# Attention and a tanh-shrink layer on one core: the projection by seven half-size products from tile 6 on, and 25 other constants of a hand-planned schedule

## The chip, the cores and the metric

The kernel runs on one core of a Trainium2 chip. A core has TensorE (PE in the profile; PEld is its weight load, which overlaps the products), VectorE (DVE), ScalarE (ACT), GpSimd (POOL) and SyncE (SP), which run at the same time and wait for each other by semaphores. SP, ACT and POOL also issue DMA transfers, each over a ring (queue) of its own. The metric is the device time of one execution in microseconds; the time of a kernel is the median of its runs.

## What is computed

Four batches of eight heads, 768 tokens, 64 numbers a head. Half of the heads (the retrieval heads; which ones is an input) attend causally to all earlier tokens, the others to the first 4 tokens and a window of 64. The result is a matrix x of 3072 tokens by 512, which passes through a layer of width 2048:

```
scores = scale * np.matmul(q, k.transpose(0, 1, 3, 2))
...
a = np.exp(scores)
a = a / (np.sum(a, axis=-1, keepdims=True) + 1e-09)
return np.matmul(a, v).astype(np.float32)
...
h = x @ w_in
g = h - np.tanh(h)
return (g @ w_out).astype(np.float32)
```

Everything comes in and goes out in 32-bit floats; the kernel computes its products in 16-bit floats with 32-bit sums.

## The kernel before, in words

**Tiles.** The 3072 tokens are 12 tiles of 256, three to a batch. Each tile passes through three stages. *Attention*: q and k are turned (on TensorE for the first tiles, st_T at line 1028; by DMA transposes, turn at 595, for the later ones), scores are made (st_S, products at line 1141), ACT takes the exponential (1154), DVE masks (1176, 1195, 1205), TensorE multiplies by v (st_A, 1234), DVE divides (1254, 1266, 1281), and the result is turned into xT (1298 or 1316). *H*: 64 products of 256 columns (line 1358) for h, in eight units of eight; ACT takes tanh (1370), DVE makes g (1377). Tile 2's g lies in a buffer of its own, gu; all others use two buffers gt. *Projection*: g @ w_out, which has two forms.

**The two forms of the projection.** The plain one (O_group, line 1406) takes 32 products of 512 columns, and two evictions by ACT (1390). From tile ST on (quick, 1335) it is the other (sums 1491, piece 1516, step 1633, finale_b 1675). There g of a tile and w_out are each cut into 2 x 2 blocks, and the product is built from seven half-size products ("pieces") instead of eight: 7 x 8 = 56 products of 256 columns (line 1539). Four of the pieces need sums of blocks of g, which DVE makes for each tile (line 1506, in SH parts each) into the space of the masks m4. Four need sums of blocks of w_out, which DVE makes once (combine 1452, quads 1466; line 1456): 40 instructions in TQ = 8 parts each, into t2, into the buffer t16p, into tile 2's gu, and the last eight over a block of w_out itself, so they can only run when no plain projection is left. The pieces' results are put together by takes (ACT, 1574), folds (DVE, 1593) and additions (POOL, 1604), and sent by SP (1624). A tile that is the first of its batch and goes this way is "mixed" (1338): its halves are the even and the odd tokens, so its H products read xT with a stride of two.

**The order of the work.** A planner (class Plan, line 17) gets every instruction with an engine, a cost and its dependences, in an order that the program writes down, and runs a list schedule: on each engine the instruction that can start first goes first, and among several the one written down earlier. The order it finds on each engine is the order of the program. What is written down where is set by "slots": one slot for each H unit, with the projection of the tile before beside it from tile 3 on (line 1868). Attention, loads and sums are spread over slots by constants: A2 for tile 2, CUT1 for tiles 3 to 5, LD and GA for the raw loads and the gathers of batches 2 and 3, TWHEN for the sums of w_out (the first 32 from TWHEN[0] to TWHEN[1], the last eight at TWHEN[2]). STEPS and STEPL say at which H unit of the next tile which pieces run. The sums that are written down after tile TG's first H unit wait for that unit's g (the key "at"). FILLS at line 1852 are products of ones that fill TensorE's planned gaps before 18 us, FW x 128 columns each.

**The front.** q and k of tile 0 come in two halves of four heads (load_first, 474): KRING gives the ring for each half and for q and k (S is SP, A is ACT). POOL's queue carries the rest: v, the first quarter of w_in, then q and k of tile 1 (t16p, line 560). CASTS says which engine casts each half of tile 0's q and k (1024, 1022), TE and XE which engine copies which transpose, MK which engine makes the mask of each head (A: ACT at 889, in a form whose sign the rest of the code follows; D: DVE at 899), and ME behind which half's casts the masks of heads 4 to 7 stand. in_order (573) brings tile 1's q and k into order on ACT.

Of the kernel before, what the change touches and what calls it, by code (L numbers as in the profile page):

```python
# [257 lines left out]
def kernel(  # L258
# [91 lines left out]
        ot=([128, DM], FP32), v1=([128, 2 * NG, H, D + 1], FP16), vf=([128, 4, H, D + 1], FP16),  # L350
    )
    many = []
    TE = (('DA', 'DA', 'DD', 'DA'), ('DD', 'DD', 'DD', 'DD'), ('AA', 'AD', 'AA', 'DD'))
    XE = ('DDDD', 'ADDD')
    NAMED = {"A": "ACT", "D": "DVE"}
    SV = "POOL"
    FILLS = 30
    FW = 1
    FILL_END = 18000.0
    CASTS = (('ACT','DVE'),('DVE','ACT'))  # L360
    CUT = (-4.5, -4.0, 5.25, 9.5)
    GATE = {3: (1, 0), 4: (1, 0)}
    CUT1 = (-9.0, -5.0, 2.25, 13.0)
    FLEX = 2
    ST = 7
    TQ = 8
    TG = 5
    SH = 2
    TWHEN = ((4, 0), (8, 0), (8, 1))
    STEPS = {2:(1, 4, "a"),4:( 2, 6, "e"), 5: (5, "b"), 7:(3, 7, "f")}  # L370
    STEPL = {3: (1, 4, "a"), 7: (2, 6, "e", 5, "b", 3, 7, "f")}
    TRI = ()
    SPLIT = 1 << 30
    LEAD = 4
# [1 line left out]
    ENDS = "ACT"  # L376
    QUART = 7
    LD = 14
    GA = 11
    FROM = 3  # L380
    BR = 1
    AFTER = {3: 2}
    MSL = [('vf', 0, 3, 0)]
    MSE = 'DVE'
    FRONT = "A40"
    KRING = ("SS", "AA")
    IE = ("ACT", "ACT")
    WL = (1100, 1200)
    ME = 0
    MK = "ADAADDDD"  # L390
    LATE = [('vf', 0, 3, 0)]
    BEHIND = []
    MASKS = 2
    AH = 30
    TL = (1100, 1500)
    RL = (1100, 1500)
    A2 = (5, 7)
    ORDER = (0, 't1', 'v1', 1, 2, 4, 3, 5, 't2', 'r3', 6, 7)

    def program(first):  # L400
# [904 lines left out]
        def st_X(n):  # L1305
            t, hp = divmod(n, HP)
            eng = NAMED[XE[t][hp]]
            if hp == 0:
# [26 lines left out]
        def quick(t):  # L1335
            return first and t >= ST

# [114 lines left out]
        def combine(k, h, fn, a, b, w=lambda: ()):  # L1452
# [5 lines left out]
                ),  # L1458
                r=every + [("T", x, h) for x in range(1, 5) if x != k] + [("at", TG)],
                w=[("T", k, h), *w()], port=True,  # L1460
# [27 lines left out]
        def summed(k):  # L1488
            return [("S", k, h) for h in range(SH)]

        def sums(t):
# [4 lines left out]
            for k, fn, a, b, r in (  # L1496
# [4 lines left out]
            ):  # L1501
                for h in range(SH):
                    cs = slice(h * NC // SH, (h + 1) * NC // SH)
                    op(
                        "DVE", 90 + 690 // SH,
                        lambda k=k, fn=fn, a=a, b=b, cs=cs: getattr(nc.vector, fn)(
                            out=S4[k][:, cs, :], in0=a()[:, cs, :], in1=b()[:, cs, :]
                        ),
                        r=g_[h * NFU // SH : (h + 1) * NFU // SH] + [("S", x, h) for x in r],
                        w=[("S", k, h)] + ([("m4", x) for x in range(HP)] if t == ST else []),  # L1510
                        port=True,
# [49 lines left out]
        def own(t, x):  # L1561

            if x == "A":
                return [("gu", gts[2][1], u) for u in range(NFU)] if t == ST else []
            return [("ot", unit(t, x)[1])] if ("ot", t, x) not in outs else []
# [67 lines left out]
        def step(t, i):  # L1633

            for what in (STEPS if t < NTT - 2 else STEPL).get(i, ()):
                if what == "a":
# [92 lines left out]
        def attention(t):  # L1729

            vs = visits(t)
            ts = [lambda hp=hp: st_T(t * HP + hp, TE) for hp in range(HP) if t < FROM]
            last = {}
# [18 lines left out]
        if first:  # L1752
# [11 lines left out]
            for half in range(2):  # L1764
                cast_first(half, CASTS[half])
                for n in (2 * half, 2 * half + 1):
                    st_T(n, TE)
                    if half == 0:
                        masks(n)
                if half == 0:  # L1770
                    load_v(0)
                    if ORDER[0] == 0:
                        load_w_in(0)
                if half == ME:
                    masks(2)
# [18 lines left out]
        else:  # L1794
# [6 lines left out]
            for n in range(HP):  # L1801
                st_T(n, TE)
                st_S([(n, 0)])
# [8 lines left out]
        def att_u(t):  # L1812

            seq = []
            vs = attention(t)
            seq += [lambda n=n: st_T(t * HP + n, TE) for n in range(HP)]
            for f in vs:
# [5 lines left out]
        def att_pairs(t):  # L1823
# [3 lines left out]
            for hp in range(HP):  # L1827
                n = t * HP + hp
                seq.append(lambda n=n: st_T(n, TE))
                units = [(n, gi) for gi in range(g + 1)]  # L1830
# [14 lines left out]
        for i in range(FILLS if first else 0):  # L1845
# [3 lines left out]
            def mm(wm=wm, at=at):  # L1849
                for j in range(0, P.size[at], FW):  # L1850
                    n = min(FW, P.size[at] - j)
                    nc.tensor.matmul(
# [24 lines left out]
        slot_of = {x[0][1:]: s for s, x in enumerate(slots) if x[0][0] == "H"}  # L1877
# [6 lines left out]
        if first and fast:  # L1884
            spread_over([by_rank], BR, BR)
            qs = quads()
            spread_over(qs[: 4 * TQ], slot_of[TWHEN[0]], slot_of[TWHEN[1]])
            assert TWHEN[2][0] == ST + 1
            spread_over(qs[4 * TQ :], slot_of[TWHEN[2]], slot_of[TWHEN[2]])
        spread_over(att_pairs(1) + [lambda: scale_v(1, SV)], 0, 0)  # L1890
# [2 lines left out]

        def point(h):
            t, ts = divmod(h, 2)
            return slot_of[t, 4 * ts + 3] if t >= 2 else max(0, 12 + 2 * h)

        for b in range(FLEX, NTT // NG) if first and fast else ():
            left = {}
# [4 lines left out]
            for i, vis in enumerate(vs):  # L1904
                s = point(6 * b - LEAD + i)
                for t in sorted({n // HP for n, gi in vis}):
# [3 lines left out]
                    if t != 3 or "r3" not in ORDER:  # L1910
                        spread_over([lambda t=t: load_raw(t, GATE.get(t))], s - LD, s - LD)
                    spread_over([lambda t=t: gather(t), lambda t=t: spread(t)], s - GA, s - GA + 2)
                fs = between.setdefault(s, [])
# [6 lines left out]
        for t in range(NG, FLEX * NG if first and fast else NTT):  # L1920
            b, g = divmod(t, NG)
            base = slot_of[3 * b, 0]
            cut = CUT1 if b == 1 else CUT
            lo, hi = base + cut[g], base + cut[g + 1]
# [10 lines left out]
        for s, what in enumerate(slots):  # L1935
# [4 lines left out]
            for i, x in enumerate(what):  # L1940
# [8 lines left out]
                else:  # L1949
                    t, ts, f0, f1, c0, c1 = x[1:]  # L1950
# [66 lines left out]
```

## Time and profile before

| | |
|---|---|
| runs | 227.51, 229.02, 227.60 us; median 227.60 |
| the profiled execution's own time | 229.2 us |
| its span, first to last instruction | 227.4 us |
| mean granted TensorE clock | 0.991 |
| instructions in the span | 6503 |
| moved by DMA | 35.33 MB in 104133 packets |

The page's first part gives for each engine its busy time, its share of the span and its instructions. Windows give the same for a stretch: the stretch, its length, the busy time and the number of instructions of PE, PEld, DVE, ACT and POOL, the granted TensorE clock (1.00 is full), the busy share of the DMA engines and GB/s. Groups by line read: line, engine, operation, output<-input, shapes, count | busy us, mean ns of one | idle time of the engine just before them and what ended it. The chain that ended last is followed back from the last instruction; its rows are start, length, engine or DMA, and line. In the timeline, brackets hold the idle time before an instruction and what ended it. DMA issues read: transfer, queue, operation, count, KB each, median us from issue to landing.

### The profile page before, as it was taken

The numbers are of one execution on the slowest core, as the hardware profiler recorded it, in microseconds if no ns is written. First come the engines' busy times: TensorE is split into PE (matmuls) and PEld (weight loads), VectorE is DVE, ScalarE is ACT, GpSimd is POOL, SyncE is SP. The second block draws the span as 40 slices with busy tenths as digits, with TensorE's granted clock in tenths as the row PEclk, the third lists the DMA queues.
The fourth block names the chain that finished last, engine by engine and source line by source line (L and its number), as shares of the span: only waits on it lengthen the run. The fifth ranks groups of instructions, "written<-read, shape, count | busy, mean of one in ns | idle before, by whom it ended". The sixth has DMA issues, their size and how long they took to land.

```text
span 227.4 us, 6503 instructions
## 1 busy us (share of the span) xinstructions
PE 217.9 (96%) x2439; PEld 169.7 (75%) x2439; DVE 170.2 (75%) x434; ACT 143.1 (63%) x223; POOL 111.4 (49%) x243
## 2 busy tenths in 40 slices
PE   7878999999999999999999999999999999999991
PEld 7555788788886766766766677686898888888881
DVE  5638786798775967576997654879999689787872
ACT  5835866985566878574775676486567757345310
POOL 8999353764754709677662939364022021031140
PEclk9996999999999999999999999999999999999999
DMA  6999999989899999999999999954301302202023
GB/s 176 176 184 202 197 204 225 190 176 236 195 173 217 176 209 236 150 237 201 287 181 233 191 215 227 241 110 92 95 3 52 92 0 95 47 3 92 0 95 101
DMA packets 104133, 35.33 MB, mean 155 GB/s; under 512 B 90658, under 2 KB 102434, under 8 KB 104098
## 3 DMA queue, kind: packets, MB, share of 16 engines
q1 hardware_dynamic: 85600, 26.49, 56.1%
q0 software_dynamic: 17152, 7.60, 25.6%
q10 hardware_dynamic: 1346, 0.79, 1.2%
q8 instruction: 20, 0.33, 0.6%
q14 instruction: 15, 0.12, 0.2%
HBM read 27.26 MB, written 6.29 MB: 148 GB/s over the span
## 4 chain that ended last, share of the span: by engine, by line
PE 83%; DVE 5%; DMA 4%; ACT 3%; POOL 2%; issue 1%; POOLq 0%; ACTq 0%
PE banks L1358 35%; PE banks L1416 19%; PE banks L1539 14%; PE banks L1141 7%; PE banks L1234 6%; DMA t16p<-in_k_dram 4%; DVE t L1456 2%; DVE pt L1195 1%; ACT pt L1154 1%; ACT th L1370 1%; PE banks L1041 1%; POOL v L526 1%; PE banks L1119 1%; DVE QK L1024 1%; POOL t16p L560 0%
## 5 line engine op out<-in xcount | busy, mean ns | idle before, releaser
L1358 PE MATMUL banks<-xT,win 128*128 128x256 f16 x768 | 96.9, 273 | 0.3 <-ACT ot L1390 0.3
L1358 PEld LDWEIGHTS <-win 128*128 128x128 f16 x768 | 72.9, 98 | 15.7 <-issue 1.2
L1370 ACT ACTIVATE th<-banks 128x512 f32<-128x512 f32 x96 | 57.0, 606 | 34.6 <-PE banks L1358 30.4
L1377 DVE SCALAR_TENSOR_TENSOR gt<-th,banks 128x512 f16<-128x512 f32 x88 | 59.1, 678 | 14.8 <-ACT th L1370 14.1
L1154 ACT ACTIVATE pt<-banks 128x768 f16<-128x768 f32 (+1 forms) x60 | 52.9, 926 | 13.3 <-PE banks L1141 12.5
L1416 PE MATMUL banks<-wout,gt 128*128 128x256 f16 (+1 forms) x256 | 49.5, 326 | 0.0
L682 POOL CAST t<-rawqk 128x256 f16 x72 | 29.2, 451 | 30.6 <-DMA rawqk<-in_k_dram 28.0
L1604 POOL TENSOR_TENSOR ot<-gu,ot 128x256 f32<-128x256 f32 x8 | 6.9, 860 | 51.0 <-ACT gu L1574 42.8
L1416 PEld LDWEIGHTS <-gt 128*128 128x128 f16 x256 | 23.1, 98 | 10.8 <-issue 1.2
L1266 DVE TENSOR_TENSOR x16t<-banks,rinv 128x128 f32 (+1 forms) x80 | 22.5, 284 | 0.8
L1141 PE MATMUL banks<-QK 64*128 64x128 f16 (+1 forms) x364 | 21.2, 240 | 1.1 <-DVE QK L1024 0.6
L718 POOL CAST v<-rawv 128x128 f16 x72 | 21.1, 338 | 0.0
L1154 ACT ACTIVATE ptn<-banks 128x1024 f16<-128x1024 f32 (+1 forms) x18 | 17.1, 952 | 4.6 <-PE banks L1141 4.6
L1141 PEld LDWEIGHTS <-QK 64*128 64x128 f16 x364 | 12.6, 94 | 8.9 <-issue 6.1
L1234 PEld LDWEIGHTS <-pt 128*128 128x128 f16 x420 | 16.2, 97 | 3.1 <-issue 1.0
L1234 PE MATMUL banks<-v,pt 128*128 128x65 f16 x220 | 16.7, 193 | 0.2 <-ACT pt L1154 0.2
L1539 PEld LDWEIGHTS <-m 128*128 128x128 f16 x160 | 15.4, 98 | 1.9 <-issue 0.2
L1205 DVE TENSOR_TENSOR pt<-pt,m4r 128x1024 f16<-128x1024 f16 (+1 forms) x18 | 12.6, 698 | 4.2 <-ACT pt L1154 4.2
L1176 DVE TENSOR_TENSOR ptn<-ptn,mS 128x1024 f16<-128x1024 f16 x12 | 9.0, 753 | 8.3 <-ACT ptn L1154 8.3
L1254 DVE RECIPROCAL rinv<-banks 128x4 f32<-128x4 f32 x48 | 8.4, 177 | 8.5 <-PE banks L1234 7.8
L1234 PE MATMUL banks<-vf,pt 128*128 128x65 f16 x200 | 13.0, 193 | 0.1
L1390 ACT ACTIVATE ot<-banks 128x512 f32<-128x512 f32 (+1 forms) x18 | 9.2, 511 | 5.9 <-PE banks L1416 5.7
(112 smaller groups left out, 262.9 us busy)
## 6 DMA issues: line engine op xcount, KB each, us to landing
out_dram<-ot SPq DMA_DIRECT2D x18, 256.0 KB, 2.7
rawqk<-in_q_dram SPq DMA_DIRECT2D x17, 256.0 KB, 4.1
rawqk<-in_k_dram SPq DMA_DIRECT2D x17, 256.0 KB, 4.3
rawv<-in_v_dram SPq DMA_DIRECT2D x16, 256.0 KB, 4.9
win<-in_moe_w_in_dram POOLq DMA_DIRECT2D x4, 512.0 KB, 12.5
wout<-in_moe_w_out_dram POOLq DMA_DIRECT2D x4, 512.0 KB, 13.1
out_dram<-ot SPq DMA_DIRECT2D x10, 128.0 KB, 3.1
v<-in_v_dram POOLq DMA_DIRECT2D x6, 128.0 KB, 10.2
```

The costliest lines, as they stand in the source:

```text
L682: nc.gpsimd.tensor_copy(out=c5()[:, :, :, s_ : s_ + 1, :], in_=r5()[:, :, :, at, :])
L718: nc.gpsimd.tensor_copy(out=v1s[b]()[:, g * NB : g * NB + NB, RANK[s_] : RANK[s_] + 1, 0:D], in_=rv()[:, :, at, :],)
L1141: nc.tensor.matmul(out=sc()[:, hh, o : o + nb * 128], lhsT=lhsT, rhs=QK[p_, hp, q_0 : q_0 + nb * 128], start=not added, stop=not added or ...
L1154: lambda pt=pt, sc=sc, gi=gi, wid=wid: nc.scalar.activation(out=pt()[:, :, 512 * gi : 512 * gi + wid], in_=sc()[:, :, 0:wid], func=AF.Exp, ...
L1205: nc.vector.tensor_mul(out=pv, in0=pv, in1=m)
L1234: nc.tensor.matmul(out=av()[:, i, hh, :], lhsT=pt()[:, hh, co : co + 128], rhs=vv, start=(jb == first_jb), stop=(jb == qb),)
L1266: nc.vector.tensor_mul(out=xt()[:, :, at, :], in0=av()[:, :, hh : hh + 1, 0:D], in1=rinv()[:, :, hh : hh + 1].unsqueeze(3).to_broadcast([1 ...
L1358: nc.tensor.matmul(out=ph()[:, j, :], lhsT=w_in_t[fb // 4][:, cb, f0 : f0 + 128], rhs=x, start=(cb == 0), stop=(cb == HP - 1),)
L1370: lambda: nc.scalar.activation(out=th()[:], in_=ph()[:], func=AF.Tanh, scale=1.0 / XS),
L1377: lambda: nc.vector.scalar_tensor_tensor(out=gt()[:, u * FU : (u + 1) * FU, :], in0=th()[:], scalar=-XS, in1=ph()[:], op0=ALU.mult, op1=AL ...
L1416: nc.tensor.matmul(out=po()[:, c0:c1], lhsT=gt()[:, f, ts * 128 : ts * 128 + 128], rhs=w_out_t[:, f, c0:c1], start=(f == 0), stop=(f == NF ...
L1539: nc.tensor.matmul(out=po()[:, at : at + CM], lhsT=lhs(c), rhs=rhs(c), start=c == 0, stop=c == NC - 1,)
```

## The change

Only constants change, and the schedule that the planner makes from them. ST goes from 7 to 6: tile 6 is projected by the seven pieces too, and being the first of batch 2 it becomes a mixed tile. TWHEN and TG move the sums of w_out to the slots from (tile 3, unit 4) to (6, 4), and the eight last to (7, 3). SH makes the sums of g whole, four instructions a tile, where there were eight. STEPL spreads tile 10's pieces over four H units of tile 11 where there were two. KRING sends the second half of tile 0's q over SP's ring instead of ACT's. MK and ME put all eight masks on DVE, those of heads 4 to 7 behind the second half's casts. CASTS, TE and XE exchange casts and copies between ACT and DVE. FW makes the fills 256 columns wide. A2, CUT1 and GA move attention of tiles 2 to 5 and the gathers in the slots. The number in point() is read only for tiles below 2.

```diff
-    TE = (('DA', 'DA', 'DD', 'DA'), ('DD', 'DD', 'DD', 'DD'), ('AA', 'AD', 'AA', 'DD'))
-    XE = ('DDDD', 'ADDD')
+    TE = (('DA', 'DA', 'DD', 'DD'), ('DD', 'DD', 'DD', 'DD'), ('AA', 'AD', 'AA', 'DD'))
+    XE = ('DADA', 'ADDD')
...
-    FW = 1
+    FW = 2
...
-    CASTS = (('ACT','DVE'),('DVE','ACT'))
+    CASTS = (('ACT','ACT'),('DVE','DVE'))
...
-    CUT1 = (-9.0, -5.0, 2.25, 13.0)
+    CUT1 = (-8.0, -7.0, 3.0, 13.0)
     FLEX = 2
-    ST = 7
+    ST = 6
     TQ = 8
-    TG = 5
-    SH = 2
-    TWHEN = ((4, 0), (8, 0), (8, 1))
+    TG = 4
+    SH = 1
+    TWHEN = ((3, 4), (6, 4), (7, 3))
     STEPS = {2:(1, 4, "a"),4:( 2, 6, "e"), 5: (5, "b"), 7:(3, 7, "f")}
-    STEPL = {3: (1, 4, "a"), 7: (2, 6, "e", 5, "b", 3, 7, "f")}
+    STEPL = {1: (1, 4, "a"), 3: (2, 6, "e"), 5: (5, "b"), 7: (3, 7, "f")}
...
-    GA = 11
+    GA = 9
...
-    KRING = ("SS", "AA")
+    KRING = ("SS", "SA")
...
-    ME = 0
-    MK = "ADAADDDD"
+    ME = 1
+    MK = "DDDDDDDD"
...
-    A2 = (5, 7)
+    A2 = (4, 8)
...
-            return slot_of[t, 4 * ts + 3] if t >= 2 else max(0, 12 + 2 * h)
+            return slot_of[t, 4 * ts + 3] if t >= 2 else max(0, 14 + 2 * h)
```

## The prediction

> **What bounds the kernel now.** I read the page's busy shares first, then the stretches of the span, then the chain that ended last, and last the groups by line where a step needed a price.
>
> ```profile
> PE 217.9 (96%) x2439; PEld 169.7 (75%) x2439; DVE 170.2 (75%) x434; ACT 143.1 (63%) x223; POOL 111.4 (49%) x243
> PE 83%; DVE 5%; DMA 4%; ACT 3%; POOL 2%; issue 1%; POOLq 0%; ACTq 0%
> ```
>
> TensorE is busy for 217.9 of 227.4 us and holds 83% of the chain. A busy share alone doesn't say that it works at its rate, since overlapping matmuls count as busy, so the chain's pieces must give the rate.
>
> ```profile
> 6.30 10.02 DMA t16p<-in_k_dram
> 16.34 0.63 ACT t L1022
> 18.17 0.76 PE banks L1141 x10
> 18.93 0.96 PE banks L1041 x8
> 20.43 0.85 PE banks L1119 x2
> 21.28 0.76 PE banks L1358 x4
> 22.04 0.49 PE banks L1141 x10
> 24.48 0.43 PE banks L1119 x2
> 30.73 0.44 PE banks L1358 x4
> 38.74 0.57 PE banks L1041 x8
> 49.78 2.50 DVE t L1456 x8
> 53.84 0.96 DVE t L1456
> 144.74 3.02 PE banks L1416 x14
> 176.14 1.75 PE banks L1539 x16
> 185.02 1.81 PE banks L1358 x16
> 194.67 1.75 PE banks L1358 x16
> 212.14 10.49 PE banks L1539 x96
> ```
>
> Start, length, what. Three regions follow. Up to 18 us the chain waits for data: k of tile 1 is issued at 6.30 and lands 10.02 us later. From 18 to 56 us TensorE's pieces alternate with DVE's and ACT's, among them the first sums of w_out (49.78, 53.84). From there on it is TensorE's own work: a 256-column product every 1.75/16 = 0.109 us, a 512-column one every 3.02/14 = 0.216 us. So behind 56 us a microsecond of matmul removed is worth a microsecond, as long as no other engine falls behind.
>
> ```profile
> 3.00:14.00 11.00, 9.84 (x117) 6.63 (x115) 8.26 (x28) 7.17 (x13) 10.84 (x15) 1.00 1.60 210
> 15.00:18.40 3.40, 1.36 (x19) 0.96 (x19) 1.06 (x4) 2.20 (x5) 2.70 (x4) 1.00 1.36 202
> 18.40:21.80 3.40, 3.40 (x29) 2.27 (x23) 3.24 (x11) 1.78 (x3) 3.39 (x5) 0.50 1.34 201
> 140.00:152.00 12.00, 12.00 (x137) 9.00 (x136) 7.39 (x21) 8.41 (x15) 6.40 (x16) 1.00 0.92 188
> 152.00:164.00 12.00, 12.00 (x126) 8.85 (x123) 11.18 (x33) 6.99 (x12) 4.01 (x14) 1.00 0.44 101
> 164.00:180.00 16.00, 16.00 (x201) 13.59 (x196) 14.87 (x35) 11.03 (x17) 2.90 (x3) 1.00 0.19 51
> 180.00:222.60 42.60, 42.60 (x442) 37.73 (x440) 33.54 (x71) 19.84 (x33) 8.18 (x10) 1.00 0.16 48
> ```
>
> Stretch and length, then busy time of PE, PEld, DVE, ACT, POOL, the granted clock, the DMA share and GB/s. Between 15.00 and 18.40 TensorE works 1.36 us of 3.40, and in the next 3.40 us its clock is 0.50. From 140 on it is never idle, and DVE is the engine that comes next: 11.18 of 12.00 between 152 and 164.
>
> The profiled execution took 229.2 us, 1.8 around a span of 227.4. The runs shown are 227.51, 227.60 and 229.02, so it lies 1.6 above their median. I work out differences in the profile and set them against 227.6.
>
> **The change part by part.**
>
> *Tile 6's projection on TensorE.* Out go 32 products of 512 columns, 32 x 0.216 = 6.90 us. In come seven pieces of eight 256-column products, 56 x 0.109 = 6.13 us: a gain of 0.77. Tile 6 is the first tile of its batch, so its H products now read their tokens with a stride, as tile 9's do: 1.81 us for 16 (185.02) in place of 1.75 (194.67). Tile 6 has 64 of them: 4 x 0.06 = 0.24 us lost. Together -0.53 us, all of it on the path.
>
> *Tile 6's sums, folds and takes.* The four sums, two folds (E and F), two takes and three POOL additions are new; two evictions on ACT go.
>
> ```profile
> L1506 DVE TENSOR_TENSOR m<-gt 128x512 f16<-128x512 f16 x20 | 8.6, 440 | 0.0
> L1506 DVE TENSOR_TENSOR m<-gt,m 128x512 f16<-128x512 f16 x10 | 5.7, 575 | 0.0
> L1506 DVE TENSOR_TENSOR m<-m,gt 128x512 f16<-128x512 f16 x10 | 5.5, 565 | 0.1
> L1593 DVE SCALAR_TENSOR_TENSOR ot<-banks,gu 128x512 f32<-128x512 f32 x4 | 2.8, 692 | 1.4 <-PE banks L1539 1.4
> L1456 DVE TENSOR_TENSOR wout<-wout 128x256 f16<-128x256 f16 x8 | 2.1, 282 | 0.0
> L1604 POOL TENSOR_TENSOR ot<-gu,ot 128x256 f32<-128x256 f32 x8 | 6.9, 860 | 51.0 <-ACT gu L1574 42.8
> ```
>
> The sums cost (8.6 + 5.7 + 5.5)/5 = 4.0 us a tile in halves and at most that in whole pieces (SH 1 issues four instructions for eight). With two folds of 0.69 DVE gains 5.4 us. The eight instructions that overwrite a block of w_out (T1, 2.1 us) come a tile earlier too, from 161 us to about 145; they are moved, not added. Between 140 and 180 DVE is busy 7.39 + 11.18 + 14.87 = 33.44 of 40.00 us, so 6.56 are free, 4.61 of them between 140 and 152, where tile 6's sums can first run. 5.4 fits in 6.56, and behind 180 there are 9.06 more. I cost it at nothing; that cover gone it costs what the first rival has. POOL's three additions (0.86 each) lie where POOL has 5.60 of 12.00 free or more. With SH 1 no sum starts before the whole tile's g is there: at the end, the last tile's first three pieces (24 x 0.109 = 2.6 us, free of sums) and two of tile 10's (1.75) stand in front of the first piece that reads one, and the sum it reads is the second of four, about 2 us in. Nothing.
>
> *Tile 10's pieces in four places instead of two* (STEPL). The 96 pieces at the end (212.14) become 56 or a few more, and the rest run between tile 11's H products. The same work on an engine that is never idle: nothing.
>
> *w_out's sums between tiles 3 and 6.* 32 instructions are now spread over 24 slots, not 32. Those written down before tile TG's first H wait for nothing but data: eight or nine before (the trace shows 8 at 49.78 and one at 53.84, before tile 4 begins), six or seven now. So two fewer stand on DVE among tile 2's masks, up to 0.96 + 2.50/8 = 1.27 us of the chain. But what TensorE can win there is what it stood idle:
>
> ```profile
> 40.00:50.00 10.00, 9.72 (x138) 7.83 (x136) 8.45 (x19) 9.42 (x17) 6.69 (x19) 1.00 1.06 176
> 50.00:60.00 10.00, 9.94 (x145) 8.36 (x143) 8.11 (x24) 6.94 (x11) 5.50 (x12) 1.00 1.02 223
> ```
>
> That is 0.28 + 0.06 = 0.34 us. Between 0 and -0.34 I take -0.1, near zero, since the masks that they stand beside remain late.
>
> *The front: casts, masks, copies, the ring.* Head masks: three go from ACT to DVE (0.54 us each below, 1.6 in all), four of the eight now behind the second half's casts. Both casts of the first half go to ACT, both of the second to DVE; three copies change engine. The second half of q is issued third on SP's queue instead of second on ACT's; behind it on SP nothing waits before the raw loads. ACT's own k is then issued one DMA earlier.
>
> ```profile
> 17.02 0.51 PE L1041 MATMUL banks<-ident,t 128*128 128x128 f16 x6 [1.39 <-ACT t L1022]
> L899 DVE TENSOR_SCALAR m<-A,thr 128x512 f16<-128x512 f16 x5 | 2.5, 537 | 0.0
> rawqk<-in_q_dram ACTq DMA_DIRECT2D x1, 256.0 KB, 4.2
> ```
>
> Tile 0 has slack: TensorE stands 1.39 us in front of tile 1's transposes (17.02), and that wait ends with the k that took 10.02 us through POOL's queue, whose order the change leaves alone. DVE has 11.00 - 8.26 = 2.74 us free between 3 and 14. 1.6 us more fit, and if they all came late, 1.6 - 1.39 = 0.2 us would show. DVE's casts of the second half wait for both, and the transposes of heads 4 to 7 for those. The ring: one place in a queue of four is at most a quarter of a 4.2 us landing, 1.0 us either way, again in front of that wait of 1.39. I take 0 for the front, since the wait covers each of the two, and +1.2 (0.2 + 1.0) if both come together; below, 0, since POOL's queue alone sets its end.
>
> *Fills of 256 columns.* They fill gaps that the planner leaves and end before 18 us; same columns in half the instructions: 0, unless they change the clock (second rival).
>
> *Tile 2 over slots 4 to 8, batch 1's cuts, gathers two slots later.* Order alone. The raw loads keep their place (batches 2 and 3) or move two slots earlier (tile 4) or one later (tile 5), and POOL waits on them in any case. I take 0; below, the 0.34 already counted; above, one visit of tile 2 laid bare (third rival). The changed constant in point() is only read for tiles below 2, which no caller reaches: nothing.
>
> Sum: -0.53 - 0.1 = -0.6 us; 229.2 would become 228.6 in the profile, and 227.6 becomes **227.0**.
>
> **The rivals.**
>
> *DVE becomes the bound between 140 and 180 (slower).* For it: 11.18 of 12.00 is full, and sums beside a working POOL are dearer (the same add is 440 or 575). Against: 4.61 us lie free just where the new sums become ready. If only half of the 6.56 can be used, 5.4 - 3.3 = 2.1 us are left over and TensorE waits for them: -0.6 + 2.1, 229.1. It decides once less than 4.8 us can be used, for then 0.6 is eaten.
>
> *The half clock.* In the profile it costs, by the chain's pieces at 0.50 and later at 1.00, 0.76 - 0.49 (L1141), 0.96 - 0.57 (L1041), 0.85 - 0.43 (L1119) and 0.76 - 0.44 (L1358): 1.4 us. It follows the stretch with 1.36 of 3.40 busy. If the changed front keeps TensorE busier there (tile 0 later, H pushed towards 18), it is gone; if the median of before was without it and that of after has it, it is paid. The 1.5 us between the runs 227.51 and 229.02 is of this size, an estimate of mine. So 227.0 + 1.4 = 228.4 or 227.0 - 1.4 = 225.6.
> The Trainium skill, TensorE: Matmul & The Clock Gate, section on the HAM clock gate, says that activity is judged in free-running windows of about 3.4 us and an idle one halves the clock. The trace agrees in the length, 3.40 us at 0.50. By that rule the phase, not the kernel, picks the run that pays, and the sum stays at 227.0 give or take 1.4; by the row alone a shorter gap would always save it, 225.6.
>
> *An early visit of tile 2 or 3 is laid bare (slower).* Tile 3's attention is now put into one slot instead of four, tile 2's over four instead of two.
>
> ```profile
> L1154 ACT ACTIVATE pt<-banks 128x1024 f16<-128x1024 f32 x30 | 30.7, 1032 | 5.9 <-PE banks L1141 5.9
> L1195 DVE SCALAR_TENSOR_TENSOR pt<-m,pt 128x512 f16<-128x512 f16 x8 | 5.4, 711 | 1.0 <-ACT pt L1154 1.0
> ```
>
> One visit's exponential and two masks are 1.03 + 2 x 0.71 = 2.45 us; wholly exposed once they give 227.0 + 2.45 = 229.5. Against it: TensorE has H products of tiles 0 and 1 to put between, and idles only 0.34 us there now.
>
> **How the numbers follow.** Saving comes through, 226.4 to 227.8: 0.50. DVE the bound, 229.1: 0.17. Half clock paid, 228.4: 0.13; spared, 225.6: 0.08. Visit laid bare, 229.5: 0.12. The likeliest gives 227.0. The range reaches from 225.6 to 229.2 and leaves out the dearer half of the third rival, what DVE may cost beyond its price, and a little below: 0.2. One per cent, about what a measurement can tell here from no change, is 2.3 us: 225.3 and 229.9. Below the first lies half of the spared clock with some of the early gains, 0.08; above the second half of the last rival (0.06) and the dear end of DVE's (5.4 us at most, 0.10): 0.16; between them 0.76.
>
> **What would show it.** L1416 with 128 instead of 160 products of 512 columns, L1539 with 336 in place of 280, and H pieces of tile 6 at 1.81 for 16, show the first term. DVE between 140 and 180 near 38 of 40 with PE still full shows that its new work is hidden; PE idle there shows the first rival. The clock's row around 18 to 22 shows the second. PE idle over 0.34 us between 40 and 60 shows the third. The forecast is wrong if k of tile 1 lands much earlier or later than 16.34, since the whole order hangs on it.

## The result, and the profile after

| | before | changed |
|---|---|---|
| median of 22 runs each, us | 227.92 | 229.67 |
| lowest to highest, us | 226.71 to 229.16 | 227.56 to 231.06 |
| changed / before, 95% interval | | 1.0066 (1.0048 to 1.0083) |
| the profiled execution, and its span, us | 229.2, 227.4 | 229.73, 227.8 |

The changed kernel is slower by 0.66%, 1.5 us (1.1 to 1.9), where 0.6 us less was forecast. The ratio is that of the fast runs (one of the changed kernel's 22, 231.06 us, is slow) and not that of the two medians. 229.67 lies above the range; set against the 227.60 from which the forecast was made, 0.66% more is 229.1, which lies inside it, but the sign is wrong either way. The page of the changed kernel, busy shares and the chain by engine:

```profile
PE 217.3 (95%) x2439; PEld 169.8 (75%) x2439; DVE 177.0 (78%) x422; ACT 141.8 (62%) x221; POOL 114.2 (50%) x246
PE 68%; DVE 9%; DMA 4%; ACT 2%; POOL 2%; issue 1%; POOLq 0%; SPq 0%
```

TensorE's 217.3 for 217.9 is no saving: the 217.9 hold the half clock, and a second profile of the kernel before (E4 below), which has none, shows 216.4. DVE has 6.8 us more to do (170.2 before, 169.9 in E4). Its share of the chain is 9% for 5%, but 5% again in a second profile of the changed kernel (E15). The stretches of the changed kernel, columns as in the prediction:

```profile
15.00:18.40 3.40, 2.86 (x36) 1.93 (x33) 3.08 (x9) 2.49 (x5) 3.38 (x5) 1.00 1.26 206
18.40:21.80 3.40, 3.31 (x44) 2.38 (x44) 2.99 (x13) 2.72 (x5) 3.40 (x5) 1.00 1.36 202
60.00:82.00 22.00, 21.75 (x241) 16.63 (x239) 15.61 (x35) 14.94 (x23) 12.47 (x37) 1.00 1.19 209
82.00:100.00 18.00, 17.62 (x197) 11.54 (x195) 15.06 (x39) 12.82 (x19) 13.68 (x34) 1.00 1.22 222
140.00:152.00 12.00, 10.54 (x132) 8.71 (x130) 12.00 (x26) 7.28 (x12) 7.59 (x17) 1.00 0.88 156
152.00:164.00 12.00, 12.00 (x140) 10.56 (x138) 11.53 (x31) 7.04 (x12) 5.28 (x10) 1.00 0.37 89
164.00:180.00 16.00, 16.00 (x190) 13.69 (x189) 13.72 (x29) 10.85 (x17) 2.46 (x3) 1.00 0.19 51
180.00:222.60 42.60, 42.60 (x453) 37.74 (x452) 31.98 (x58) 20.24 (x33) 8.11 (x10) 1.00 0.19 53
```

Three stretches in which TensorE never stood idle before now have idle time: 0.25 (60 to 82), 0.38 (82 to 100) and 1.46 us (140 to 152), 2.09 in all. From 140 to 152 DVE is busy without a break, 12.00 of 12.00. Less the 0.53 us that were forecast for the projection, 2.09 makes 1.56, and 1.5 were measured; that the sum comes out so well is partly luck, for E15 has 0.76, 0.04 and 0.80, 1.60 in all, with about the same loss (0.60%). The half clock of the first profile is gone.

What DVE does from 138.59 on, and TensorE's waits in the same place (the timeline of the changed kernel):

```profile
138.59 0.69 DVE L1377 SCALAR_TENSOR_TENSOR gt<-th,banks 128x512 f16<-128x512 f32 x1 [0.50 <-ACT th L1370]
139.31 2.52 DVE L1506 TENSOR_TENSOR m<-gt 128x1024 f16<-128x1024 f16 x1
141.76 0.70 DVE L1456 TENSOR_TENSOR wout<-wout 128x256 f16<-128x256 f16 x1
142.39 0.68 DVE L1506 TENSOR_TENSOR m<-m,gt 128x1024 f16<-128x1024 f16 x1
142.99 0.37 DVE L1456 TENSOR_TENSOR wout<-wout 128x256 f16<-128x256 f16 x1
143.28 0.68 DVE L1506 TENSOR_TENSOR m<-gt,m 128x1024 f16<-128x1024 f16 x1
143.88 0.80 DVE L1176 TENSOR_TENSOR ptn<-ptn,mS 128x1024 f16<-128x1024 f16 x1
```

```profile
144.74 0.20 PE L1234 MATMUL banks<-vf,ptn 128*128 128x65 f16 x1 [0.54 <-DVE ptn L1176]
147.86 0.52 PE L1141 MATMUL banks<-QK 64*128 64x128 f16 x10 [0.24 <-DVE gt L1377]
148.94 1.03 PE L1539 MATMUL banks<-wout,gt 128*128 128x256 f16 x8 [0.56 <-DVE gt L1377]
```

Tile 6's first sum comes at 139.31; it and the next four, three of the g sums (L1506) and two of the eight that overwrite a block of w_out (L1456), stand in front of the mask at 143.88 for which TensorE waits at 144.74. The later waits are for g itself. The 0.38 us between 82 and 100 is the same on a smaller scale, in the chain that ended last:

```profile
89.53 0.68 DVE gt L1377
90.22 3.26 DVE t L1456 x7
93.48 0.71 DVE ptn L1176
94.18 0.05 issue
94.23 0.30 PE banks L1234 x4
```

Tile 4's first g (89.53) releases every sum of w_out that waits for it; seven run in a row, and a mask behind them is late.

### The profile page after: what moved, and what is told of

Its sections match the earlier page's. It is cut to its first block, busy times and chain, and to the rows that moved or that the text cites. A ratio compares the mean times of both kernels' runs of the same rounds, so it can differ in the third digit from the quotient of the medians.

```text
span 227.8 us, 6483 instructions
## 1 busy us (share of the span) xinstructions
PE 217.3 (95%) x2439; PEld 169.8 (75%) x2439; DVE 177.0 (78%) x422; ACT 141.8 (62%) x221; POOL 114.2 (50%) x246
## 4 chain that ended last, share of the span: by engine, by line
PE 68%; DVE 9%; DMA 4%; ACT 2%; POOL 2%; issue 1%; POOLq 0%; SPq 0%
PE banks L1358 27%; PE banks L1416 15%; PE banks L1539 15%; PE banks L1141 5%; PE banks L1234 5%; DMA rawqk<-in_k_dram 2%; DMA QK<-t 2%; DVE gt L1377 2%; DVE m L1506 2%; DVE t L1456 1%; DVE pt L1195 1%; POOL t L682 1%; ACT pt L1154 1%; DVE wout L1456 1%; POOL v L718 1%
## 5 line engine op out<-in xcount | busy, mean ns | idle before, releaser
L1154 ACT ACTIVATE pt<-banks 128x768 f16<-128x768 f32 (+1 forms) x60 | 52.8, 920 | 11.7 <-PE banks L1141 10.6
L682 POOL CAST t<-rawqk 128x256 f16 x72 | 29.7, 462 | 30.3 <-DMA rawqk<-in_k_dram 30.3
L1416 PE MATMUL banks<-wout,gt 128*128 128x256 f16 (+1 forms) x224 | 42.4, 318 | 0.2 <-DVE gt L1377 0.2
L1604 POOL TENSOR_TENSOR ot<-gu,ot 128x256 f32<-128x256 f32 x10 | 8.9, 887 | 52.0 <-ACT gu L1574 39.6
L1416 PEld LDWEIGHTS <-gt 128*128 128x128 f16 x224 | 20.1, 98 | 7.4 <-issue 1.0
L1539 PEld LDWEIGHTS <-m 128*128 128x128 f16 x192 | 18.5, 98 | 2.5 <-issue 0.2
L1539 PEld LDWEIGHTS <-gt 128*128 128x128 f16 x144 | 13.7, 98 | 2.2 <-issue 0.7
L1539 PE MATMUL banks<-wout,gt 128*128 128x256 f16 x96 | 12.8, 273 | 0.6 <-DVE gt L1377 0.6
```

The lines of the kernel that those rows point to most:

```text
L682: nc.gpsimd.tensor_copy(out=c5()[:, :, :, s_ : s_ + 1, :], in_=r5()[:, :, :, at, :])
L1154: lambda pt=pt, sc=sc, gi=gi, wid=wid: nc.scalar.activation(out=pt()[:, :, 512 * gi : 512 * gi + wid], in_=sc()[:, :, 0:wid], func=AF.Exp, ...
L1416: nc.tensor.matmul(out=po()[:, c0:c1], lhsT=gt()[:, f, ts * 128 : ts * 128 + 128], rhs=w_out_t[:, f, c0:c1], start=(f == 0), stop=(f == NF ...
L1539: nc.tensor.matmul(out=po()[:, at : at + CM], lhsT=lhs(c), rhs=rhs(c), start=c == 0, stop=c == NC - 1,)
```

## The experiments

Two theories stood at first. *Theory 1*: DVE's new work between 140 and 152 us eats the projection's saving and more. *Theory 2*: the loss comes from the front and the order. The runs soon added a question: does the front cost on the chip, or through the planner, which gets other costs and so finds another order much later? "Idle" is TensorE's idle time in a window of one profile.

**The change in three parts (E1 to E3) and the kernel before once more (E4).** E1 takes ST, TG, SH, TWHEN and STEPL from the changed kernel, E2 the front (KRING, CASTS, TE, XE, MK, ME, FW), E3 the rest (A2, CUT1, GA).

```diff
E1, before with the changed kernel's
+ ST = 6; TG = 4; SH = 1; TWHEN = ((3, 4), (6, 4), (7, 3)); STEPL
E2, before with the changed kernel's
+ KRING; CASTS; TE; XE; MK; ME; FW
E3, before with the changed kernel's
+ A2 = (4, 8); CUT1; GA = 9
```

> The kernel before with the projection's constants alone (ST, TG, SH, TWHEN, STEPL). Theory 1 (DVE jams when tile 6's sums and the eight instructions over w_out arrive together, and TensorE waits): ratio 1.005 to 1.010, TensorE idle 1 us or more between 138 and 155 us. Theory 2 (the slow part is the front or the order of the early attention, the projection itself gains its 0.5 us): ratio 0.996 to 0.999, TensorE without idle time there.

> The kernel before with the front's constants alone (KRING, CASTS, TE, XE, MK, ME, FW). Theory 1: ratio 0.994 to 1.001, since the changed profile shows the front done 1.4 to 2 us earlier than the profile before. Theory 2: ratio above 1.003.

> The kernel before with the places of attention and gathers alone (A2, CUT1, GA). Theory 1: ratio 0.998 to 1.002. Theory 2: above 1.003, with TensorE idle over 0.34 us between 40 and 60 us.

> The kernel before once more, for a second profile of it. If the half clock between 18 and 22 us comes and goes from run to run, this profile can be without it, and its span is then 1.4 us shorter, near 226.0; if the kernel always pays it, the span is 227.4 again.

| | ratio to before, 95% | idle 60 to 82 | 82 to 100 | 136 to 156 |
|---|---|---|---|---|
| E1 projection | 1.0009 (0.9985 to 1.0033) | 0.38 | 0.61 | 0.73 |
| E2 front | 1.0035 (1.0006 to 1.0064) | 0.79 | 0 | 0 |
| E3 order constants | 1.0016 (0.9985 to 1.0047) | 0 | 0 | 0 |
| E4 before | one run, 226.79 us | 0 | 0 | 0 |

The idle time at 136 to 156 belongs to the projection, that at 60 to 82 mostly to the front. None of the three alone makes the 0.66%. E1's ratio lies between the ranges of the two theories, E2's is that of theory 2, E3's that of theory 1, although E3 has 0.65 us idle between 40 and 60. E4 has no half clock; its front, windows:

```profile
15.00:18.40 3.40, 2.63 (x37) 1.91 (x35) 2.71 (x8) 2.19 (x4) 3.38 (x5) 1.00 1.30 206
18.40:21.80 3.40, 3.23 (x42) 2.15 (x40) 3.40 (x13) 2.31 (x4) 3.40 (x5) 1.00 1.36 201
```

The same program has TensorE busy for 2.63 us here where the first profile had 1.36, and the next 3.40 us run at full clock. Its span is 224.9 us, 2.5 less than the first profile's and not only 1.4: besides the half clock, TensorE stands idle for 0.77 us between 15.00 and 18.40 where it was 2.04. In none of the 19 later profiles, of either kernel or an experiment, is the front at half clock.

**All but the front (E5); parts of the front (E6, E7); the sums in halves (E8).**

```diff
E5, the changed kernel without
- KRING; CASTS; TE; XE; MK; ME; FW
E6, before with
+ KRING = ("SS", "SA"); CASTS = (('ACT','ACT'),('DVE','DVE'))
E7, before with
+ ME = 1; MK = "DDDDDDDD"
E8, E1 with
+ SH = 2
```

> The changed kernel with the front's seven constants as before. If the front carries over half of the slow-down wherever it stands (theory F, from the run of the front alone, 1.0035): ratio 1.001 to 1.004. If the projection's wait on DVE carries it and the front's figure was chance (theory P): ratio 1.005 to 1.008, still with 1 us or more of TensorE idle between 136 and 156 us.

> The kernel before with KRING and CASTS alone. If the ring is what the front costs: ratio 1.002 to 1.006. If the masks on DVE or the order that the planner makes of the rest do: 0.998 to 1.002.

> The kernel before with MK and ME alone (all eight masks on DVE, four of them behind the second half's casts). If the masks are what the front costs: ratio 1.002 to 1.006, with tile 0's first scores later than 7.55 us. If the ring does: 0.998 to 1.002.

> The projection's constants alone as in the first experiment, but SH 2 as before, so that each sum of g is two instructions. If the wait at 139 to 152 us comes from one long sum that POOL's work stretches (2.52 us in the changed profile for an instruction that elsewhere takes 0.68): ratio 0.003 below the first experiment's, so 0.996 to 0.999, and TensorE idle under 0.4 us there. If it comes from the amount of DVE's work: ratio as there or above (1.000 to 1.004), for halves cost DVE 0.3 us a tile more, with TensorE idle as before.

E5 gave 1.0035 (1.0019 to 1.0050), idle 0.75 at 136 to 156 and none from 60 to 136: about half of the loss goes with the front (theory F), half stays. E7 gave 1.0021 (0.9997 to 1.0044), with tile 0's first scores at 8.47: not told from none. E8 gave 1.0032 (1.0002 to 1.0061), idle 0.69 at 136 to 156: that the sums are whole is not the cause. Of its two expectations the one for a long sum fell and the one for the amount of work came in; but E1, with which it is compared, has no such long sum at that place either (0.71, 1.10 and 0.68 us). E6 was the surprise, outside both expectations: 1.0191 (1.0167 to 1.0214), 4.3 us, more than the whole front with which it shares both edits. Its front was not late; TensorE idled 2.65 us between 100 and 136 instead, mostly in front of H products, some 90 us after the casts.

**Chip or planner (E9, E10).** In E9 the planner is told the old ring and engines, so its order stays; the instructions that are written use the new ones. E10 is the mirror image.

```diff
E9, from before:
-  lambda x=x, src=src, hs=hs, ring=ring: engs[ring].dma_start(
+  lambda x=x, src=src, hs=hs, ring="SP" if (half, x) == (1, 0) else ring: engs[ring].dma_start(
...
-  def fn(x=x, e=e):
+  def fn(x=x, e=("ACT", "DVE")[half]):
E10, from E6:
-  lambda x=x, src=src, hs=hs, ring=ring: engs[ring].dma_start(
+  lambda x=x, src=src, hs=hs, ring="ACT" if half else "SP": engs[ring].dma_start(
...
-  def fn(x=x, e=e):
+  def fn(x=x, e=(("ACT", "DVE"), ("DVE", "ACT"))[half][x]):
```

> The planner is told the old ring and the old engines of the four first casts, so that its list of instructions keeps the order of the kernel before from 29 us on; the chip gets the new ring (second q half over SyncE) and the new engines (both casts of the first half on ScalarE, both of the second on VectorE). Theory A (the +4.4 us of the run with ring and casts alone come from the planner's other order 100 us later): ratio to before 0.997 to 1.004, about 227.7 us, TensorE idle between 100 and 136 us under 0.5 us. Rival B (the ring or the casts cost this on the chip itself): ratio 1.015 to 1.022, about 232 us, idle of 2 us or more between 100 and 136 us.

> The mirror image: the planner is told the new ring and the new engines of the casts, the chip gets the old ones. Theory A (the order is the cost): ratio 1.015 to 1.022, about 232 us, with TensorE gaps near 102, 112, 118 and 125 us that sum to 2 us or more, as with ring and casts changed for both. Rival B (the chip's own front is the cost): ratio 0.997 to 1.004, about 227.7 us.

E9 gave 0.9994 (0.9971 to 1.0016), E10 1.0221 (1.0186 to 1.0256). Windows of E9, windows of E10, and TensorE's waits in E10's timeline:

```profile
100.00:120.00 20.00, 20.00 (x212) 13.90 (x211) 17.87 (x54) 12.73 (x20) 11.59 (x31) 1.00 1.10 224
120.00:136.00 16.00, 16.00 (x168) 11.17 (x167) 10.13 (x25) 10.55 (x15) 9.07 (x22) 1.00 1.01 196
```

```profile
100.00:120.00 20.00, 18.25 (x208) 12.09 (x207) 13.88 (x43) 12.49 (x19) 11.72 (x34) 1.00 1.27 197
120.00:136.00 16.00, 15.07 (x170) 10.63 (x168) 14.78 (x40) 11.62 (x17) 11.75 (x26) 1.00 1.22 209
```

```profile
102.53 1.03 PE L1358 MATMUL banks<-xT,win 128*128 128x256 f16 x8 [0.44 <-ACT ot L1390]
113.02 1.03 PE L1358 MATMUL banks<-xT,win 128*128 128x256 f16 x8 [0.39 <-DVE x16t L1266]
118.97 1.91 PE L1358 MATMUL banks<-xT,win 128*128 128x256 f16 x16 [0.92 <-DVE gt L1377]
125.36 1.03 PE L1358 MATMUL banks<-xT,win 128*128 128x256 f16 x8 [0.63 <-DVE gt L1377]
```

With the old order the new ring and casts cost nothing that these runs can tell; with the new order the old ring and casts cost 2.2%. For E6 this settles it: the loss is in the order alone. The planner's own end (self.end in Plan.run, which adds up the costs it was given and is no chip time) knows of it: 220.57 us for before, 226.38 for E6, 220.57 for the whole front of E2, 221.69 for E1, 221.60 for the changed kernel, 1.0 us more than for before. It is a coarse sign: 222.80 for E8, which is 0.3% slower, and 220.99 for E14 below, which is 1.2% slower.

**How much of DVE's work (E11, E12).** E11 is E1 with the last eight sums of w_out made over 8 of their 256 columns, in the same place of the order. E12 is E1 with these sums spread over slots 3 to 6 of tile 7 and piece 5 at step 7.

```diff
E11, combine:
+  wd = 8 if k == 1 else CM
-  out=T_(k)[:, cs, :], in0=a()[:, cs, :], in1=b()[:, cs, :]
+  out=T_(k)[:, cs, 0:wd], in0=a()[:, cs, 0:wd], in1=b()[:, cs, 0:wd]
E12:
-  spread_over(qs[4 * TQ :], slot_of[TWHEN[2]], slot_of[TWHEN[2]])
+  spread_over(qs[4 * TQ :], slot_of[TWHEN[2]], slot_of[ST + 1, 7])
+  STEPS = {2: (1, 4, "a"), 4: (2, 6, "e"), 7: (5, "b", 3, 7, "f")}
```

> The projection part alone (tile 6 on by seven products), with the eight sums of the last block of w_out written over 8 of their 256 columns only, in the same place of VectorE's order; so that block isn't summed, about 3 us of VectorE's work between 139 and 152 us is left out, and all else stays. Theory A (the amount of VectorE's work that arrives together there eats the gain): TensorE idle between 136 and 156 us falls from 0.73 us to 0.3 us or less, ratio 0.996 to 1.000 where the full form had 1.0009 (about 227.2 us). Rival B (the masks wait because of the sums of tile 6 and the gather beside them, not for these eight): idle stays at 0.6 to 0.8 us and the ratio at 1.000 to 1.003.

> The projection part alone, with the eight sums of the last block spread over the slots 3 to 6 of tile 7 instead of all at slot 3, and piece 5 moved from step 5 to step 7. Theory A (VectorE's burst is the cost): TensorE idle between 136 and 156 us is 0.4 us or less, ratio 0.996 to 0.9995, about 227.1 us: this form would beat both kernels. Rival B (the work only moves, and piece 5 or a mask waits later): idle of 0.6 us or more between 136 and 165 us, ratio 1.000 to 1.004.

E11 gave 0.9980 (0.9959 to 1.0000): -0.5 us by the medians of the spans in one call (225.1 against 225.6). E12 gave 1.0107 (1.0071 to 1.0143). Windows of E1, E11 and E12:

```profile
136.00:156.00 20.00, 19.27 (x224) 15.82 (x220) 18.97 (x48) 11.98 (x19) 15.96 (x39) 1.00 0.82 157
```

```profile
136.00:156.00 20.00, 19.66 (x235) 16.49 (x234) 18.72 (x48) 11.97 (x20) 15.00 (x36) 1.00 0.76 143
```

```profile
136.00:156.00 20.00, 18.84 (x224) 15.24 (x223) 18.88 (x45) 11.39 (x18) 13.76 (x34) 1.00 0.73 140
```

The eight sums by group, in E1 and in E11:

```profile
L1456 DVE TENSOR_TENSOR wout<-wout 128x256 f16<-128x256 f16 x8 | 3.3, 410 | 0.0
```

```profile
L1457 DVE TENSOR_TENSOR wout<-wout 128x8 f16<-128x8 f16 x8 | 2.7, 339 | 0.0
```

Over 8 columns the eight instructions still take 2.7 us where they took 3.3, so E11 leaves out 0.6 us of DVE's work and not the 3 us that were expected. The idle time falls by 0.39 us all the same (0.73 to 0.34). DVE is hardly less busy (18.72 for 18.97), also because more of the later work falls into the window: TensorE has 235 instructions in it, 224 in E1. The ratios of E1 and E11 differ by 0.29%, which is not clear of noise (their two intervals together allow about 0.32%, an estimate), so E11 alone doesn't show that the amount of DVE's work is the cause. Moving the sums later (E12) was slower than either expectation, with 1.16 us idle, 0.50 of it a new wait for g at 154.70; this idle time does not account for 1.07%, 2.4 us.

**The same sums earlier, and the changed kernel again (E13 to E15).** Seven of the eight sums need not overwrite w_out: four chunks fit in the rest of gu, three in a new tile of 1.5 KB a partition, all made between tiles 5 and 6. E13 does this in E5, E14 in the changed kernel.

```diff
+ t1_t = w_pool.tile([128, 3, CM], FP16, name="t1")
...
+ def T1_(c):
+     return gts[2][0]()[:, NC + 4 + c, :] if c < 4 else t1_t[:, c - 4, :] if c < 7 else W_(0, 1)[:, c, :]
...
- spread_over(qs[4 * TQ :], slot_of[TWHEN[2]], slot_of[TWHEN[2]])
+ spread_over(qs[4 * TQ : -1], slot_of[5, 0], slot_of[6, 4])
+ spread_over(qs[-1:], slot_of[TWHEN[2]], slot_of[TWHEN[2]])
```

> The changed kernel with the front constants of before (its full form had the ratio 1.0035 and 0.75 us of TensorE's idle time between 136 and 156 us), in which seven of the eight sums of the last block go to memory that is free from tile 2 on (four to the rest of the buffer that holds the third block, three to a new tile) and are made between tiles 5 and 6; the eighth stays in place. Theory A (VectorE's burst of sums eats the projection's gain): idle between 136 and 156 us 0.3 us or less, ratio 0.997 to 1.001, about 227.4 us. Rival B (the sums of tile 6 and the gather beside them hold the masks up, the eight sums don't matter, or the earlier place makes a new wait at 100 to 136 us): idle of 0.6 us or more somewhere between 80 and 156 us beyond that of the full form, ratio 1.002 to 1.006.

> The changed kernel whole, with the same seven sums made early. Theory A: ratio 1.000 to 1.004 where the changed kernel has 1.0066, idle between 136 and 156 us 0.5 us or less. Rival B: ratio 1.005 to 1.008, idle of 0.9 us or more there.

> The changed kernel once more, unaltered. If the order sets the idle time at 136 to 156 us: 1.2 to 1.7 us again. If it is the one profile's: 0.6 to 1.1 us, as with the old front. In both cases the ratio is 1.005 to 1.008, about 229 us; a ratio under 1.004 would mean that the first measurement overstated the loss.

E15 gave 1.0060 (1.0037 to 1.0083), idle 0.80 at 136 to 156: the 1.46 was the one profile's, the loss is not. E13 gave 1.0107 (1.0071 to 1.0142) and E14 1.0120 (1.0077 to 1.0164), though idle there fell to 0.27 in both. Here seven of the eight instructions are really gone from the place, and DVE, busy for 12.00 of 12.00 us between 140 and 152 in E1, E5, E8 and E15, is so for 11.40 and 11.41: the idle time there comes of DVE's work. Inside the span E14 is 1.1 us shorter than E15 (medians 225.95 and 227.05; before 225.5). But the time outside the span, about 1.9 us elsewhere, is about 4.1 us in all twelve of their runs.

**Four sums earlier without a new tile (E16, E17); the tile alone (E18).** E16 is E5 with four of the sums in gu and the 32 others from slot (4, 4) on, E17 the changed kernel with the same four, E18 the kernel before with the tile, which nothing uses.

```diff
E16, E17:
+ def T1_(c):
+     return gts[2][0]()[:, NC + 4 + c, :] if c < 4 else W_(0, 1)[:, c, :]
...
- spread_over(qs[4 * TQ :], slot_of[TWHEN[2]], slot_of[TWHEN[2]])
+ spread_over(qs[4 * TQ : -4], slot_of[5, 0], slot_of[6, 4])
+ spread_over(qs[-4:], slot_of[TWHEN[2]], slot_of[TWHEN[2]])
E16 also:
+ TWHEN = ((4, 4), (6, 4), (7, 3))
E18:
+ t1_t = w_pool.tile([128, 3, CM], FP16, name="t1")
```

> The changed kernel with the front constants of before, four of the eight sums of the last block made early into the free rest of the buffer that holds the third block, the other four in place, no new tile; the 32 early sums start at slot 4 of tile 4. If VectorE's burst is the cost and the time outside the span is 1.9 us again: span 225.0 to 225.9 us, ratio 0.997 to 1.002, idle of TensorE at 136 to 156 us 0.5 us or less. If the sums made early cost the time outside the span, and not the tile: ratio 1.008 to 1.012 again.

> The changed kernel whole, with the same four sums made early, no new tile. Burst theory: median span 0.4 to 1.1 us under the 227.05 us of the changed kernel, ratio 1.000 to 1.004 with 1.9 us outside the span. Rival (four sums less in the burst change nothing): ratio 1.005 to 1.008. If the early place costs the time outside the span: ratio 1.010 to 1.014.

> The kernel before with the added tile of 1.5 KB in each partition that nothing reads or writes. If the tile (where the memory of the others comes to lie) costs the time outside the span: about 4.1 us there and a ratio of 1.008 to 1.011. If it doesn't: 1.9 us and a ratio of 0.998 to 1.002; then the cause lies in the instructions.

E16 gave 1.0038 (1.0021 to 1.0055), idle 0.27 at 136 to 156; E17 1.0092 (1.0058 to 1.0125), idle there 0.14, but 0.89 at 60 to 82, 0.38 at 82 to 100 and a new 0.47 behind 156. E18 gave 1.0019 (0.9986 to 1.0053) and 1.86 us outside the span: the tile alone is not what costs 2.2 us there, and that stays open. E16 and E17 have 1.7 to 2.1 us outside the span. No version with tile 6 by seven products that computes the whole result beats the kernel before: with some of the sums made early the idle time at 136 to 156 falls to 0.14 to 0.27, but the time isn't won. E13 and E14 lose it outside the span and E17 idles elsewhere. E16 is no faster than E5 (1.0035), but it moves the 32 other sums as well and so is no clean test of the four; where it loses isn't found, for its idle time in all windows (0.28 at 30 to 45, 0.46 at 45 to 60, 0.02 at 82 to 100, 0.27 at 136 to 156) doesn't explain 1.0038.

## Why the prediction was wrong, step by step

**The projection's term, -0.53, was counted right, but only about half of it is seen.** Eight H products of tile 6 in the chain of the changed kernel, and the plain form's 512-column products by group:

```profile
132.56 0.91 PE banks L1358 x8
```

```profile
L1416 PE MATMUL banks<-wout,gt 128*128 128x512 f16 x96 | 25.6, 379 | 0.0
L1416 PE MATMUL banks<-wout,gu 128*128 128x512 f16 x32 | 8.1, 380 | 0.0
```

96 + 32 = 128 products of 512 columns are left, as forecast, and eight of tile 6's H products take 0.91, or 1.82 for 16 (1.81 was assumed). What this is worth on TensorE can be had from the traces: take each product from its start to the next one's start, less idle time, behind 30 us. All products of lines 1358, 1416 (512 columns) and 1539 together then take 144.25 to 144.61 us in seven profiles with tile 6 by the plain form and 143.90 to 144.40 in the eleven with the pieces (the first profile and E10, which have more H products behind 30 us, left out): in the mean about 0.3 us less, where 0.53 were counted. E11's -0.5 us (-0.9 to 0) fits either figure.

**The step that failed is DVE's cover: "5.4 fits in 6.56 ... I cost it at nothing", and with it "they are moved, not added".** The prediction added up free time over 40 us, but the work comes in 12 of them, in which 4.61 us were free. Even this depends on where the window lies: in E4, whose work stands 2 us earlier there for want of the half clock (tile 4's first g at 89.07, not 91.10), the same 12 us have 2.45 free:

```profile
140.00:152.00 12.00, 12.00 (x125) 8.38 (x122) 9.55 (x27) 7.21 (x13) 7.04 (x19) 1.00 0.83 165
```

Into these go the sums of tile 6, 3.3 us by the groups below ((11.7 + 4.1 + 4.1)/6 tiles), and the eight sums of w_out, 3.1 us. Moved out of 152 to 164 is moved *into* 140 to 152; together 6.4 us for 4.61. The groups of the changed kernel:

```profile
L1506 DVE TENSOR_TENSOR m<-gt 128x1024 f16<-128x1024 f16 x12 | 11.7, 978 | 0.2
L1506 DVE TENSOR_TENSOR m<-m,gt 128x1024 f16<-128x1024 f16 x6 | 4.1, 683 | 0.0
L1506 DVE TENSOR_TENSOR m<-gt,m 128x1024 f16<-128x1024 f16 x6 | 4.1, 679 | 0.0
L1456 DVE TENSOR_TENSOR wout<-wout 128x256 f16<-128x256 f16 x8 | 3.1, 389 | 0.0
```

The sign given for the first rival came in: from 140 to 180 DVE is busy for 37.25 of 40.00 us, and TensorE is idle there. The rival had the mechanism, at 0.17, with 2.1 us for the wait; 0.69 to 1.46 were idle at 136 to 156 in the five profiles with all these sums in place (E1, E5, E8, E15 and the changed kernel), none in the profiles with tile 6 by the plain form, save 0.24 in E6 and E10. That its 229.1 is 1.5 us above 227.6, as measured, is luck, since about half of the loss goes with the front, of which it knows nothing. It "decides once less than 4.8 us can be used" of 40 us; the count that decides is that of the 12. That the idle time comes of DVE's work is shown (E13, E14, E16, E17); that it is all of the 0.35% that stay without the front is not, since E16 has 0.27 us of it left and is no faster.

**"Order alone. I take 0" failed as a rule.** Here the order constants of E3 cost little (0.16%, not told from none), but E10 shows that an order alone can cost 2.2%. A new number in the front changes which instruction the planner finds ready first, from there on.

**The front, 0, was right for the ring and the casts and wrong in sum.** Ring and casts cost nothing on the chip that could be told (E9). The whole front costs 0.35% (E2), and 0.66% - 0.35% (E5) = 0.31% in the changed kernel as well (about 0.1 to 0.5%, an estimate from the two intervals). Whether its other five constants cost this on the chip or through the order was not tried apart. In the changed kernel the first scores start at 8.16 instead of 7.55, and later TensorE waits for DMA transposes; a row of E15's timeline and one of E2's:

```profile
68.66 0.56 PE L1141 MATMUL banks<-QK 64*128 64x256 f16 x10 [0.54 <-DMA QK<-t]
```

```profile
68.16 0.56 PE L1141 MATMUL banks<-QK 64*128 64x256 f16 x10 [0.41 <-DMA QK<-t]
```

The six profiles with this ring and these casts on the chip other than E6's (E2, E9, E14, E15, E17 and the changed kernel) have 0.25 to 0.89 us idle between 60 and 82; of the other 14 two have any (0.28 in E7 and 0.38 in E1). E9 has 0.66 and is not slower, so this idle time alone isn't shown to be the front's price. Why the transposes land late was not tried.

**The sums of w_out, -0.1, brought nothing.** Seven run early, as counted, but the others are released together by tile 4's first g, and TensorE's idle time at 82 to 100, none in the profile before, is 0.38 us in the changed kernel, 0.04 in E15, 0.61 in E1 and none in E5, E8 and E12, all with TG = 4. **The third rival** (a visit of tile 2 or 3 laid bare for 2.45 us) didn't happen: 0.43 idle between 40 and 60, over its sign of 0.34 by little, and 0.28 in E15.

**The half clock** had no part in the loss: the profile of before had it and lay 1.6 us above its median, all later ones have not. The condition given for it, k of tile 1 late and TensorE busy for 1.36 of 3.40 us, held in that one profile alone; by the rule quoted from the Trainium skill (TensorE: Matmul & The Clock Gate, the HAM clock gate) an idle window comes before the slow one, and the traces agree in part: the stretch before it, 1.36 of 3.40 us busy, was not idle but the least busy of the 20, and of the stretches from 15.00 to 18.40 that were not followed by it the least busy has 2.16 of 3.40 (E5).

## What to carry to other kernels

Compare new work with the free time of the stretch in which it becomes ready, up to the first consumer behind it on that engine's queue, and count work moved into the stretch as added. Where a greedy planner writes the order, a constant has two prices, the instruction's own and that of the new order; telling the planner one thing and writing another separates them, and the planner's own end is worth reading before a run, as a coarse sign. An experiment that shortens an instruction has to be checked for what the instruction then takes. A gap that is closed in one place need not shorten the kernel: look at the span and the time around it, not at the gap.

## What the runs showed of the hardware that was not expected

**A sum of two operands can stand still behind GpSimd.** The sum at 139.31 took 2.52 us where its like takes 0.68. GpSimd in the timeline of the changed kernel, then DVE and GpSimd in that of E15, the same program:

```profile
138.16 1.98 POOL L718 CAST v<-rawv 128x128 f16 x8
140.08 1.21 POOL L737 TENSOR_TENSOR vf<-v,rflagr 128x260 f16<-128x260 f16 x2
```

```profile
139.35 0.84 DVE L1506 TENSOR_TENSOR m<-gt 128x1024 f16<-128x1024 f16 x1
```

```profile
138.16 2.49 POOL L718 CAST v<-rawv 128x128 f16 x8
140.62 1.68 POOL L737 TENSOR_TENSOR vf<-v,rflagr 128x260 f16<-128x260 f16 x2
```

In the first run GpSimd worked on unhindered and DVE lost 1.84 us; in E15 DVE's sum took 0.84 and GpSimd's same ten instructions took 0.51 and 0.47 us longer. From the first sum to the start of the mask behind it DVE needed 4.57 us in the one run (139.31 to 143.88) and 3.41 in the other (139.35 to 142.76). Either of the two can pay. The Trainium skill (SBUF — State Buffer, SBUF: two separate sides) says that VectorE's second port and GpSimd's are one, locked for a whole instruction, also by a VectorE instruction with two operands in SBUF; the two traces agree in that one side waits, mostly, while the other does not. In the first run the sum stood longer than for one instruction: it lasts from 139.31 to 141.83, over the last of GpSimd's casts and both of its products (to 141.29). That this is why 1.46 us stood idle in one profile and 0.80 in the other is likely, but no run isolates it.

**Time outside the span.** In E13 and E14 it is 4.02 to 4.35 and 3.96 to 4.33 us, in every other kernel 1.7 to 2.4. A spare tile alone (E18) doesn't cause it. Their pages show one packet less on an instruction queue, E13's and E15's row:

```profile
q14 instruction: 14, 0.11, 0.2%
```

```profile
q14 instruction: 15, 0.12, 0.2%
```

Whether a load of instructions that now lies outside the span costs the 2.2 us was not tried.
